# Gate row by column tiles, a new order of the opening, and remainder weight rows in three requests

## The chip, the cores and the metric

The kernel runs on one core of one Trainium2 chip. The metric is the device time of one execution in microseconds (us). TensorE (PE in the profile) multiplies, PEld is its weight load, VectorE is DVE, ScalarE is ACT, GpSimd is POOL, and SyncE (SP) issues most of the transfers (DMAs).

## What is computed

```python
mod = (silu(c) @ w_mod).reshape(1, 6, 1, 576)     # sa, ca, ga, sb, cb, gb
h = layernorm(x) * (1 + ca) + sa
x = x + ga * attention(h)      # 32 heads of 18; 8 keys per position, 2 apart, backwards
h = layernorm(x) * (1 + cb) + sb
x = x + gb * (((h @ w_gate) * (h @ w_up)) @ w_down)   # 576 -> 4608 -> 576
```

x has 2048 rows of 576 columns; everything is bfloat16 with float32 sums.

## The kernel before, in words

The 2048 rows are cut into 8 chunks of 256 rows (two halves j of 128). The attention of a chunk is: layernorm, transpose, q, k and v (`a_q`, `a_v`), products of q with shifted k (`b_p`, in the opening `pj`), their sums by head (`b_l`, `lj`), a softmax over 8 positions, and the weighted sum of shifted v. v goes to DRAM (`vd`) and comes back shifted (`b_ld`). For chunk 0 alone the shift is made on TensorE: `shift_attn` shifts the attention weights, `av_mul` multiplies, `av_sum` shifts back and adds. Half 1 needs 16 rows of half 0 as well: constants `edge` and `edge_t`, the weights `ash_e` and the values `v_e`.

The MLP works on groups of chunks, [[0], [1, 2], [3, 4], [5, 6], [7]]. `gate_up` loops over f, 36 tiles of 128 hidden columns; `down` multiplies by w_down. 576 = 4 x 128 + 64, so the last 64 rows of w_gate and w_up, the remainder rows, are kept apart in `wgr`: gate in partitions 0 to 63, up in 64 to 127, 4608 columns each, loaded by `load_wgr` (L158) in two requests of 64 rows. A `Pair` (L708, its matmuls are issued by L706) runs gate on the lower 64 rows of TensorE and up on the upper 64 at the same time, then swaps. The other 512 rows come in blocks of 4 f (`load_wgu`, L146): blocks 0 to 2 in the opening, block 3, used from f = 12, into the tile hh.

What sets the order: every engine and every DMA queue does its instructions in the order of the code, and they wait for each other by semaphores. The opening (L1020 to L1218) is an order written out by hand. From `gate_up` on, pieces of the next chunks' attention are put between the f tiles by a planner (`timed`), from costs and due times in tuples: (TensorE cost, VectorE cost, needs, mark, wait, call).

The change touches these places. `mod_row` (L349) makes a row ga or gb, copied to all 128 partitions by a 128-column stationary operand: 5 matmuls of 512 columns, 5 of 64, two ScalarE copies to float32 (L358, L359). ga is made in the opening from `wmC`; gb in the first `gate_up`, from `wm5` and `wm5r`. `mod_columns` (L321) makes the other rows by four matmuls at a time, each in 32 columns of the array. `sum_j` (L1090) is softmax's sum, reciprocal and product for a half of chunk 0. `b_wj` (L577) is chunk 0's output projection. `norm_act` (L283) is a layernorm on ScalarE. `pet` (L1143) are seven small matmuls that turn `edge` into `edge_t`.

Of the kernel before, what the change touches and what calls it, by code (L numbers as in the profile page):

```python
# [18 lines left out]
P = 128  # L19
# [9 lines left out]
FT = FF // P  # L29
HALO = 16  # L30
# [8 lines left out]
VR = H - VA  # L39

# [4 lines left out]
def kernel(  # L45
# [31 lines left out]
    vstage = pool("vstage", 2)  # L77
# [25 lines left out]
    ga_bc = consts.tile([P, D], F32, name="ga_bc")  # L103
    gb_bc = consts.tile([P, D], F32, name="gb_bc")
# [4 lines left out]
    wgr = wts.tile([P, FF], BF, name="wgr")  # L109
# [5 lines left out]
    vd = dramp.tile([HALO + S, D], BF, name="vd")  # L115
    prod_t = consts.tile([P, 4 * KT * CH], BF, name="prod_t")
# [41 lines left out]
    def load_wgr():  # L158
        for t, wsrc in enumerate((B_w_gate, B_w_up)):
            r = nc.sync.dma_start(wgr[64 * t:64 * (t + 1), :], wsrc[KF * P:D, :])  # L160
        return r
# [66 lines left out]
    for k in range(2):  # L228
# [11 lines left out]
    edge = sp.tile([HALO, W - 1, P], BF, name="edge")  # L240
# [4 lines left out]
    nc.gpsimd.affine_select(out=edge[:], in_=edge[:], compare_op=ALU.not_equal, fill=1.0, base=-2,  # L245
                            pattern=[[-(HALO + DIL), W - 1], [1, P]], channel_multiplier=-1)
    nc.gpsimd.affine_select(out=edge[:], in_=edge[:], compare_op=ALU.is_ge, fill=0.0, base=SPAN - 1,
                            pattern=[[-DIL, W - 1], [0, P]], channel_multiplier=-1)
    nc.gpsimd.memset(wo[64:, KF, :], 0.0)
# [10 lines left out]
    def ln_parts(src, tag, act=False, both=None):  # L260
        stats = small.tile([P, ST, 2, 6], F32, name="ln_stats" + tag)
        mv = small.tile([P, ST, 2], F32, name="ln_mv" + tag)
        rstd = small.tile([P, ST], F32, name="ln_rstd" + tag)
        xn = xns[turn[0] % 2]
        turn[0] += 1
        both = tag == "b" if both is None else both

        def stat(j, hfs=(0, 1)):
            for hf in hfs:
                nc.vector.bn_stats(stats[:, j, hf, :], src(j)[:, hf * 288:(hf + 1) * 288])  # L270
            if hfs[-1] == 1:
                nc.vector.bn_aggr(mv[:, j, :], stats[:, j, :, :].rearrange("p a b -> p (a b)"))

        def rsq(r):
            nc.scalar.activation(rstd[:, r], mv[:, r, 1], ACTF.Ln, bias=eps[:])
            nc.scalar.activation(rstd[:, r], rstd[:, r], ACTF.Exp, scale=-0.5)

        def norm(j):
            for d0, s0, n in ((0, 0, D), (D, D - 64, 64))[0:2 if both else 1]:
                nc.vector.tensor_scalar(xn[:, j, d0:d0 + n], src(j)[:, s0:s0 + n], mv[:, j, 0:1], rstd[:, j:j + 1],  # L280
                                        ALU.subtract, ALU.mult)

        def norm_act(j):  # L283
            nb = small.tile([P, 1], F32, name="ln_nb")
            nc.vector.scalar_tensor_tensor(nb[:], mv[:, j, 0:1], -1.0, rstd[:, j:j + 1], ALU.mult, ALU.mult)
            for d0, s0, n in ((0, 0, D), (D, D - 64, 64))[0:2 if both else 1]:
                nc.scalar.activation(xn[:, j, d0:d0 + n], src(j)[:, s0:s0 + n], ACTF.Identity, bias=nb[:], scale=rstd[:, j:j + 1])
        return xn, stat, rsq, (norm, norm_act) if act is None else norm if not act else norm_act
# [60 lines left out]
    def mod_row(wm, dst):  # L349
        pa = ps([P, 512], F32, "pa")  # L350
        pb = ps([P, 64], F32, "pb")
        for p_t, c0, c1 in ((pa, 0, 512), (pb, 512, D)):
            for kt in range(KT):
                m = wm(kt)
                rows = slice(0, m.shape[0])
                nc.tensor.matmul(p_t[:], lhsT=sc_bc[rows, kt, :], rhs=m[:, c0:c1],
                                 start=(kt == 0), stop=(kt == KT - 1))
        nc.scalar.copy(dst[:, 0:512], pa[:])  # L358
        nc.scalar.copy(dst[:, 512:D], pb[:])  # L359
# [176 lines left out]
    def shift_attn(j):  # L536
        pz = ps([P, W, H], F32, "pz")
        for w in range(W):
            o = SPAN + DIL * (W - 1 - w)
            nc.tensor.matmul(pz[:, w, :], lhsT=shifts[:, o:o + P], rhs=attn0[:, j, w, :], start=True, stop=True)  # L540
        ashs[j] = sp.tile([P, W, H], BF, name=f"ash{j}")
        nc.scalar.copy(ashs[j][:], pz[:])
        if j > 0:
            pzb = ps([P, H], F32, "pzb")
            for w in range(W - 1):
                nc.tensor.matmul(pzb[:], lhsT=edge[:, w, :], rhs=attn0[0:HALO, j, w, :], start=(w == 0), stop=(w == W - 2))
            nc.scalar.copy(ash_e[:], pzb[:])
        bb[0]["vsh"][j] = vshp.tile([P, W, DH, H], BF, name="vsh")
# [9 lines left out]
    def av_sum(j, hf, acc={}):  # L558
        if hf == 0:
            acc[j] = (ps([P, KF, P], F32, "po"), ps([P, P], F32, "po4"))  # L560
        po, po4 = acc[j]
        v = bb[0]["vsh"][j][:].rearrange("p w d h -> p w (d h)")
        dst = [(po[:, m, :], m * P) for m in range(KF)] + [(po4[:], D - P)]
        for w in range(4 * hf, 4 * hf + 4):
            o = SPAN - DIL * (W - 1 - w)
            for m, (d, c0) in enumerate(dst):
                nc.tensor.matmul(d, lhsT=v[:, w, c0:c0 + P], rhs=shifts[:, o:o + P], start=(w == 0 and m in (0, KF)),  # L567
                                 stop=(w == W - 1), skip_group_check=True)
        if hf == 1:
            if j > 0:  # L570
                for d, c0 in dst:
                    nc.tensor.matmul(d[:, 0:HALO], lhsT=v_e[:].rearrange("p d h -> p (d h)")[:, c0:c0 + P], rhs=edge_t[:],
                                     start=False, stop=True, skip_group_check=True)
            nc.scalar.copy(oT[:, 0:KF, js(j)], po[:])
            nc.scalar.copy(oT[0:64, KF, js(j)], po4[64:P, :])

    def b_wj(j):  # L577
# [10 lines left out]
        def rest(stat):  # L588
            for hf, (cs, pw) in enumerate(pws):
                nc.vector.tensor_tensor(xt[:, cs], pw[:], ga_bc[:, cs], ALU.mult)  # L590
                nc.vector.tensor_tensor(xt[:, cs], xt[:, cs], x_res[0][:, j, cs], ALU.add)
                stat(j, (hf,))
        return rest
# [138 lines left out]
    def wg_pair(gi, hh, f, part):  # L732
# [6 lines left out]
        def side(t):  # L739
            def ops(rows, k):  # L740
                if k == KF:
                    return wgr[rows, js(f)], ht[rows, KF, :]
# [18 lines left out]
        return Pair(("pg", "pu"), N, (side(0), side(1)), finish)  # L761
# [253 lines left out]
    def load_wm5():  # L1015
        nc.gpsimd.dma_start(wm5(), w_mod[0:KF * P, 5 * D:6 * D].rearrange("(k p) n -> p k n", p=P))
        nc.gpsimd.dma_start(wm5r[0:64, :], w_mod[KF * P:D, 5 * D:6 * D])
# [70 lines left out]
    ashs = {}  # L1088

    def sum_j(j):  # L1090
        ss = small.tile([P, H], F32, name="ssj")
        nc.vector.tensor_reduce(ss[:], dd0[:, j].rearrange("p w h -> p h w"), axis=AX.X, op=ALU.add)
        nc.vector.reciprocal(ss[:], ss[:])
        nc.vector.tensor_tensor(attn0[:, j], dd0[:, j], ss[:, None, :].to_broadcast([P, W, H]), ALU.mult)

    load_wm(wmC, 2, 1)
    for dd4 in range(4):
        nk = (DH - dd4 + 3) // 4
        wsrc = bass.AP(A_wo.tensor, A_wo.offset + dd4 * D, [[DH * D, H], [4 * D, nk], [1, D]])
        nc.sync.dma_start(wo[dd4 * H:(dd4 + 1) * H, 0:nk, :], wsrc)  # L1100
    load_res(0)
    load_wm_tail(wmB, 3)
    nc.sync.dma_start(wmB[:, 0:KF, :], w_mod[0:KF * P, 3 * D:5 * D].rearrange("(k p) n -> p k n", p=P))
    load_x(2)
    load_wgr()
    for g in range(3):
        load_wgu(g)
    cp, dv = nc.scalar.copy, nc.vector.tensor_copy
# [32 lines left out]
    pet = ps([P, HALO], F32, "pet")  # L1141
    for w in range(W - 1):
        nc.tensor.matmul(pet[:], lhsT=edge[:, w, :], rhs=ident[0:HALO, 0:HALO], start=(w == 0), stop=(w == W - 2))  # L1143
    nc.scalar.copy(edge_t[:], pet[:])
    mod_row(lambda k: wmC[:, k, :], ga_bc)
    for w in range(4):
        lj(1, w)
    sum_j(0)
    a_q(1, 0)
    shift_attn(0)  # L1150
    for w in range(4, 8):
        pj(1, w)
    a_q(1, 1)
    for w in range(4, 8):
        lj(1, w)
    av_mul(0, 0)
    max_j(1)
    a_q(1, 2)
    av_mul(0, 1)
    sum_j(1)  # L1160
    a_q(1, 3)
    av_sum(0, 0)
    a_q(1, 4)
    av_sum(0, 1)
    shift_attn(1)
# [3 lines left out]
    xn2, stat2, rsq2, norm2 = ln_parts(lambda j: x1[0][j], "b")  # L1169
    stat2c(0)  # L1170
    stat2c(1)
    rsq2c(slice(0, 2))
    av_mul(1, 0)
    x1_halves = []

    def products_1():
        x1_halves.append(b_wj(0))
        norm2c(0)
        norm2c(1)
        a_v(1, 0)  # L1180

    add_modc = mod_columns(wmB, 1, products_1)
    x1_half = x1_halves[0]
    av_mul(1, 1)
    edge_mul()
    add_modc()
    av_sum(1, 0)
    x1_half(stat2)
    a_t(2, False)
    av_sum(1, 1)  # L1190
    b_p(1, 0)
    rsq2(slice(0, 1))
    a_v(1, 1)
# [17 lines left out]
    a_v(2, 0)  # L1211
    b_l(1, 0)
    for w in range(4, 8):
        b_p(1, w)
    a_v(2, 1)
# [41 lines left out]
    def gb_row():  # L1257
        mod_row(lambda k: wm5()[:, k, :] if k < KF else wm5r[0:64, :], gb_bc)
# [3 lines left out]
    first = [(0, 0, "", "p17", 1.4, nop), (0.75, 0, "p17", "l14", 1.0, lambda: b_l(1, 4)), (0.35, 0, "l14", "t14", 0.3, lambda: b_lt(1))] + first  # L1262
# [8 lines left out]
               [[(0, 0, "", "-", 0, lambda: (load_wm5(), load_wd(0))), (0, 0, "", "z3", 8.0, both_halves), (0, 0, "", "w5", 12.0, nop), (1.5, 0, "w5", "-", 0, gb_row), (0, 0, "", "-", 0, lambda: load_res(2))],  # L1271
# [3 lines left out]
                                         (0.6, 0.8, "n4 v3", "x4", 0, lambda: (a_t4(), load_x(6)))]]),  # L1275
# [84 lines left out]
```

## Time and profile before

| | us |
|---|---|
| median of 3 runs | 544.71 |
| lowest and highest | 543.72, 546.1 |
| the profiled execution, by its own time | 544.44 |
| its span (first to last instruction) | 542.7 |
| mean granted TensorE clock | 1.00 of full |
| TensorE busy in the first 130 us | 127.44 |
| DMA rate, 24 to 27, 27 to 36 and 36 to 41 us | 415, 217 and 356 GB/s |

How to read it: an engine's busy time is the sum of its instructions' spans; matmul ends are modelled. The chain is followed back from the last instruction, at each step to what released it; its lines give start, length and what ran. A line of waits says who waited for whom, the total, how often. A line of issues gives the tile, the queue, the size and the median time from issue to landing. A queue's line gives packets, megabytes and the share of 16 DMA engines' time. L numbers are lines of the kernel.

### The profile page before, as it was taken

What the parts mean: (1) busy time and instruction counts of PE and PEld (TensorE: products, weight loads), DVE (VectorE), ACT (ScalarE), POOL (GpSimd) and SP (SyncE); (2) the same over time, 40 slices, a digit from 0 to 9 for tenths busy, and PEclk for the clock granted to TensorE, in tenths of its full rate; (3) what the DMA queues carried; (4) which work ended last, traced back from release to release, by engine and by line L of the source; (5) the groups of instructions that cost most, each with busy time, mean ns of one, the idle gap of its engine ahead of it and who ended that gap; (6) DMA issues with size and microseconds to landing.
All of it is one profiled execution on the core that took longest, in us unless ns stands there. A gap on an engine that the chain in (4) does not pass through costs nothing.

```text
span 542.7 us, 14569 instructions
## 1 busy us (share of the span) xinstructions
PE 535.3 (99%) x6157; PEld 321.9 (59%) x6189; DVE 315.9 (58%) x713; ACT 251.5 (46%) x617; POOL 67.9 (13%) x104
## 2 busy tenths in 40 slices
PE   8999999999999999999999999999999999999997
PEld 4887789756745444555544444555544445558875
DVE  4989586777766777646358896524344924032212
ACT  4776777543566553022645552014555551006630
POOL 7104012122000110111000110110010101010210
PEclk9999999999999999999999999999999999999999
DMA  8999999778872694878435983894296592849821
GB/s 264 299 261 363 336 272 332 258 224 258 267 203 89 211 208 153 227 220 293 135 108 163 232 288 68 162 239 159 89 275 176 156 311 69 255 138 294 271 74 42
DMA packets 94924, 114.52 MB, mean 211 GB/s; under 512 B 27980, under 2 KB 83676, under 8 KB 94732
## 3 DMA queue, kind: packets, MB, share of 16 engines
q1 hardware_dynamic: 83360, 67.29, 44.6%
q0 software_dynamic: 11344, 46.25, 27.8%
q8 instruction: 48, 0.79, 0.6%
q14 instruction: 16, 0.13, 0.1%
q10 hardware_dynamic: 156, 0.07, 0.0%
HBM read 103.15 MB, written 4.74 MB: 199 GB/s over the span
## 4 chain that ended last, share of the span: by engine, by line
PE 94%; DMA 3%; DVE 1%; SPq 1%; ACT 1%; issue 0%
PE pg L706 28%; PE pu L706 23%; PE acc L921 19%; PE pq L706 3%; PE accr L926 3%; PE pw L605 3%; PE pq L416 3%; PE acc L976 3%; PE lgT L470 2%; DMA wmC<-in_w_mod_dram 2%; PE pv L706 2%; PE pv L439 1%; DMA wqk<-in_A_wqkv_dram 1%; PE po L567 1%; PE pwj L584 0%
## 5 line engine op out<-in xcount | busy, mean ns | idle before, releaser
L706 PE MATMUL pg<-h2T,wgu 64*128 64x512 bf16 (+1 forms) x1376 | 265.5, 331 | 0.0
L706 PE MATMUL pu<-h2T,wgu 64*128 64x512 bf16 (+1 forms) x1376 | 264.5, 331 | 0.0
L706 PEld LDWEIGHTS <-wgu 64*128 64x128 bf16 x2752 | 136.5, 94 | 94.8 <-issue 0.5
L757 ACT CAST u_sb<-pu 128x512 bf16<-128x512 f32 (+1 forms) x172 | 85.4, 497 | 135.8 <-PE pg L706 131.2
L760 DVE TENSOR_TENSOR hh<-g_sb,u_sb 128x512 bf16<-128x512 bf16 x136 | 57.4, 423 | 116.2 <-ACT g_sb L758 115.7
L758 ACT CAST g_sb<-pg 128x512 bf16<-128x512 f32 (+1 forms) x172 | 86.7, 504 | 0.0
L921 PEld LDWEIGHTS <-hh 128*128 128x128 bf16 x504 | 49.0, 98 | 59.5 <-issue 1.5
L921 PE MATMUL acc<-wd,hh 128*128 128x512 bf16 x329 | 84.1, 380 | 0.1
L926 PE MATMUL accr<-wd,hh 128*128 128x64 bf16 x344 | 62.4, 193 | 0.7
L706 PE MATMUL pu<-h2T,wgr 64*128 64x512 bf16 (+1 forms) x188 | 61.5, 327 | 0.2 <-ACT u_sb L757 0.2
L706 PE MATMUL pg<-h2T,wgr 64*128 64x512 bf16 (+1 forms) x188 | 61.5, 327 | 0.0
L926 PEld LDWEIGHTS <-hh 128*128 128x128 bf16 x504 | 45.8, 98 | 1.9
L171 POOL DMA_DIRECT2D wd<-in_B_w_down_dram x29 | 21.8, 752 | 190.0 <-PE accr L926 93.4
L461 DVE TENSOR_TENSOR prod_t<-qT,kT 128x1280 bf16<-128x1280 bf16 x56 | 43.7, 818 | 0.7 <-ACT kT L777 0.7
L514 DVE TENSOR_TENSOR vsh<-vsh,attn 128x1152 bf16<-128x1152 bf16 x56 | 39.6, 748 | 1.2 <-DMA vsh<-vd 1.2
L706 PEld LDWEIGHTS <-wgr 64*128 64x128 bf16 x376 | 19.7, 94 | 15.4 <-issue 2.5
L921 PE MATMUL acc<-prod_t,hh 128*128 128x512 bf16 x111 | 28.8, 380 | 0.0
L304 ACT ACTIVATE h2T<-h2T,modc 128x256 bf16<-128x256 bf16 x12 | 6.6, 595 | 45.3 <-DMA h2T<-xn 45.3
L455 POOL DMA_DIRECT2D vsh<-vd x14 | 12.5, 897 | 104.8 <-DVE o_sb L524 89.6
L706 PE MATMUL pq<-hT,wqk 64*128 64x256 bf16 (+1 forms) x360 | 22.2, 259 | 0.1
L416 PE MATMUL pq<-hT,wqk 128*128 128x256 bf16 (+1 forms) x225 | 21.2, 251 | 0.4 <-ACT hT L304 0.4
L926 PE MATMUL accr<-prod_t,hh 128*128 128x64 bf16 x112 | 21.6, 193 | 0.1
(208 smaller groups left out, 605.0 us busy)
## 6 DMA issues: line engine op xcount, KB each, us to landing
wgu<-in_B_w_gate_dram SPq DMA_DIRECT2D x41, 512.0 KB, 4.5
wgu<-in_B_w_up_dram SPq DMA_DIRECT2D x41, 512.0 KB, 6.4
wd<-in_B_w_down_dram POOLq DMA_DIRECT2D x29, 576.0 KB, 5.6
vsh<-vd POOLq DMA_DIRECT2D x14, 1152.0 KB, 9.3
prod_t<-in_B_w_down_dram POOLq DMA_DIRECT2D x8, 576.0 KB, 7.6
hh<-in_B_w_down_dram POOLq DMA_DIRECT2D x6, 576.0 KB, 6.4
x_r<-in_A_x_dram SPq DMA_DIRECT2D x8, 288.0 KB, 8.3
vd<-v_sb POOLq DMA_DIRECT2D x16, 144.0 KB, 5.2
```

What stands on the lines that cost most here:

```text
L171: return nc.gpsimd.dma_start(wb[:], B_w_down[r0:r0 + FB * P, :].rearrange("(k p) n -> p k n", p=P))
L416: nc.tensor.matmul(pq[:, gi, :], lhsT=wqk[:, kt, m * P:(m + 1) * P], rhs=hT[:, kt, cols], start=(kt == order[0] and not (by_k and gi)), st ...
L461: nc.vector.tensor_tensor(prod, aa[i]["qT"][:], aa[i]["kT"][:, :, off:off + CH], ALU.mult)
L514: nc.vector.tensor_tensor(v, v, at, ALU.mult)
L605: nc.tensor.matmul(pw[:], lhsT=oT[:, m, js(j)], rhs=wo[:, m, 0:512], start=(m == 0), stop=(m == KT - 1))
L706: return nc.tensor.matmul(out, lhsT=lhs, rhs=rhs, start=first, stop=last, skip_group_check=True)
L757: nc.scalar.copy(u[:, c, :], pu)
L758: nc.scalar.copy(g[:, c, :], pg)
L760: return lambda: nc.vector.tensor_tensor(hh[:, f - c:f + 1, :], g, u, ALU.mult)
L921: nc.tensor.matmul(acc[j][:], lhsT=hh[:, f, js(j)], rhs=wb[:, f % FB, 0:512], start=(f == 0), stop=(f == FT - 1))
L926: nc.tensor.matmul(accr[:, j, :], lhsT=hh[:, f, js(j)], rhs=wb[:, f % FB, 512:D], start=(f == 0 and j == 0), stop=(f == FT - 1), skip_grou ...
L976: nc.tensor.matmul(acc[i][:], lhsT=hh[:, f, js(j)], rhs=wb(f)[:, c0:c1], start=(f == 0), stop=(f == FT - 1))
```

## The change

- The remainder rows: `wgr` becomes [128, 2, 2304]. The gate rows come in one request to all 128 partitions, its source read as 2 column halves x 64 rows x 2304 columns; the up rows in two requests of 64 partitions, with the halves the other way round. It is issued after weight block 1 in place of before block 0. From f = 18 on, up runs on the lower rows of TensorE and gate on the upper.
- gb is made by `gb_cols`: 20 matmuls of 144 columns, four side by side, one copy to bfloat16, then through DRAM (`gd`) and back to all partitions, on GpSimd's queue. ga keeps its way (`ga_row`). Both rows are bfloat16.
- `edge_t` is built on GpSimd by a memset and seven selects, `edge` has 128 rows in place of 16; the `pet` matmuls go.
- The reciprocal in `sum_j` becomes exp(-ln) on ScalarE, and its product is a step of its own, `share_j`.
- `norm_act`'s extra 64 columns go to VectorE.
- The opening from `pj(1, 3)` to `b_ld(1, 0)` has another order; the end of `av_sum` for half 1 is `av_out`; `load_x(2)` is issued before `load_res(0)`; `a_v(2, 1)` stands before `b_l(1, 0)`.
- `vstage` has 4 buffers in place of 2; three numbers of the planner change.

```diff
     def load_wgr():
-        for t, wsrc in enumerate((B_w_gate, B_w_up)):
-            r = nc.sync.dma_start(wgr[64 * t:64 * (t + 1), :], wsrc[KF * P:D, :])
-        return r
+        rows = slice(KF * P, D)
+        nc.sync.dma_start(wgr[:, 0, :], bass.AP(B_w_gate.tensor, B_w_gate.offset + KF * P * FF, [[FH, 2], [FF, 64], [1, FH]]))
+        nc.sync.dma_start(wgr[64:, 1, :], B_w_up[rows, 0:FH])
+        nc.sync.dma_start(wgr[0:64, 1, :], B_w_up[rows, FH:FF])
...
+    nc.gpsimd.memset(edge_t[:], 0.0)
+    for w in range(W - 1):
+        d = edge_t[:, 0:SPAN - DIL * w]
+        nc.gpsimd.affine_select(out=d, in_=d, compare_op=ALU.not_equal, fill=1.0, base=-DIL - (HALO + DIL) * w,
+                                pattern=[[-1, SPAN - DIL * w]], channel_multiplier=1)
...
-            for d0, s0, n in ((0, 0, D), (D, D - 64, 64))[0:2 if both else 1]:
-                nc.scalar.activation(xn[:, j, d0:d0 + n], src(j)[:, s0:s0 + n], ACTF.Identity, bias=nb[:], scale=rstd[:, j:j + 1])
+            nc.scalar.activation(xn[:, j, 0:D], src(j)[:, 0:D], ACTF.Identity, bias=nb[:], scale=rstd[:, j:j + 1])
+            if both:
+                nc.vector.tensor_scalar(xn[:, j, D:], src(j)[:, D - 64:D], mv[:, j, 0:1], rstd[:, j:j + 1], ALU.subtract, ALU.mult)
...
+    def gb_cols(wm):
+        pa = ps([P, GC], F32, "pa")
+        for kt in range(KT):
+            for q in range(4):
+                nc.tensor.matmul(pa[H * q:H * (q + 1), :], lhsT=sc_bc[:, kt, 0:H], rhs=wm(kt)[:, GC * q:GC * (q + 1)],
+                                 start=(kt == 0), stop=(kt == KT - 1), skip_group_check=True)
+        nc.scalar.copy(grow[:], pa[:])
+        nc.gpsimd.dma_start(gd[:], grow[0:P:H, :])
+        nc.gpsimd.dma_start(gb_bc[:], bass.AP(gd.tensor, gd.offset, [[0, P], [1, D]]))
...
-                    return wgr[rows, js(f)], ht[rows, KF, :]
+                    return wgr[rows, t, js(f % (FT // 2))], ht[rows, KF, :]
...
-        return Pair(("pg", "pu"), N, (side(0), side(1)), finish)
+        if f < FT // 2:
+            return Pair(("pg", "pu"), N, (side(0), side(1)), finish)
+        return Pair(("pu", "pg"), N, (side(1), side(0)), lambda pu, pg: finish(pg, pu))
...
-        nc.vector.reciprocal(ss[:], ss[:])
-        nc.vector.tensor_tensor(attn0[:, j], dd0[:, j], ss[:, None, :].to_broadcast([P, W, H]), ALU.mult)
+        nc.scalar.activation(ss[:], ss[:], ACTF.Ln)
+        nc.scalar.activation(ss[:], ss[:], ACTF.Exp, scale=-1.0)
+        sums[j] = ss
...
+    load_x(2)
     load_res(0)
     load_wm_tail(wmB, 3)
     nc.sync.dma_start(wmB[:, 0:KF, :], w_mod[0:KF * P, 3 * D:5 * D].rearrange("(k p) n -> p k n", p=P))
-    load_x(2)
-    load_wgr()
     for g in range(3):
         load_wgu(g)
+        if g == 1:
+            load_wgr()
...
-    pet = ps([P, HALO], F32, "pet")
-    for w in range(W - 1):
-        nc.tensor.matmul(pet[:], lhsT=edge[:, w, :], rhs=ident[0:HALO, 0:HALO], start=(w == 0), stop=(w == W - 2))
-    nc.scalar.copy(edge_t[:], pet[:])
-    mod_row(lambda k: wmC[:, k, :], ga_bc)
+    a_q(1, 0)
+    ga_row()
+    sum_j(0)
     for w in range(4):
         lj(1, w)
-    sum_j(0)
-    a_q(1, 0)
+    pj(1, 4)
+    pj(1, 5)
+    share_j(0)
+    a_q(1, 1)
     shift_attn(0)
...
+    x1_halves[0](stat2, edge_mul)
+    a_tiles(2)
+    hT2 = aa[2]["hT"]
+    ev2 = transposed(xn2c, lambda m: hT2[:, m, :], (0, 1), 0)
+    av_out(1)
+    ev2(False)
...
-    first = [(0, 0, "", "p17", 1.4, nop), (0.75, 0, "p17", "l14", 1.0, lambda: b_l(1, 4)), (0.35, 0, "l14", "t14", 0.3, lambda: b_lt(1))] + first
+    first = [(0, 0, "", "p17", 2.2, nop), (0.75, 0, "p17", "l14", 1.0, lambda: b_l(1, 4)), (0.35, 0, "l14", "t14", 0.3, lambda: b_lt(1))] + first
```

## The prediction

> **What bounds the kernel now.** I read the page's busy times first, then the chain, then the opening in the timeline and the transfers in the same stretches.
>
> ```profile
> span 542.7 us, 14569 instructions
> PE 535.3 (99%) x6157; PEld 321.9 (59%) x6189; DVE 315.9 (58%) x713; ACT 251.5 (46%) x617; POOL 67.9 (13%) x104
> ...
> PE 94%; DMA 3%; DVE 1%; SPq 1%; ACT 1%; issue 0%
> ```
>
> TensorE is busy for 99% of the span and carries 94% of the chain, at a granted clock of 1.0. So a change gains only what it takes off TensorE's own list or out of its few waits, and loses whatever new wait it gives TensorE. The chain from 20 us on, cut to its places of interest:
>
> ```profile
> 11.76 8.89 DMA wmC<-in_w_mod_dram
> 20.65 0.14 issue
> 20.79 0.38 PE pa L356
> ...
> 57.40 1.20 ACT xn L287 x2
> 58.60 0.26 ACT u_sb L757
> ...
> 62.77 0.32 PE pa L356
> ...
> 64.42 0.09 PE pu L706
> 64.50 0.13 PE pg L706 x2
> 64.64 0.28 PE pu L706
> ```
>
> Three waits stand there: for wmC until 20.79, for ScalarE's norm of chunk 3 (the next matmul starts 0.45 us after the one before it, at 58.90, where 0.11 is usual: 0.34 lost), and at 64.64, where the up half of weight block 3 has just landed. The waits name the last one, and the issues give the age of that load:
>
> ```profile
> PEld L706 <- DMA hh<-in_B_w_up_dram: 0.3, 1, 0.3
> ...
> hh<-in_B_w_up_dram SPq DMA_DIRECT2D x1, 512.0 KB, 22.9
> ```
>
> Issued at 41.67, it lands at 64.6 after 22.9 us: the queue is full. So from about 28 to 65 us the transfers keep step with TensorE with nothing to spare, and their order and speed count. The issue sections and queue lines of the first 60 us show two more things:
>
> ```profile
> q10 hardware_dynamic: 12, 0.00, 0.0%
> ...
> vd<-v_sb POOLq DMA_DIRECT2D x6, 144.0 KB, 6.0
> ...
> v_e<-vd POOLq DMA_DIRECT2D x1, 144.0 KB, 10.8
> ```
>
> q10 has carried only the three c_row requests by then. One has a leading count of 4, two of 1. Twelve packets are 6 of data and 6 of completion, 4+1+1 of each. Over the whole page q10 has 156: the 144 more are the last output request, 128 rows and 16 completions. So a request occupies as many DMA engines as its leading count allows, 16 for 128 rows. v_e is written to 128 partitions, but its source leads with a count of 8: in the packet records never more than 8 of its 32 packets are in flight (13 to 16 for vd's), and it needs 10.8 us where vd's requests of the same size need 6.0. The smaller leading count of the two sides decides.
>
> **The remainder rows.** Before, wgr comes as two requests of 64 rows by 9216 bytes. Their 128 packets mean 655 ns in the records, 5.2 us on each of 16 engines; the first ones, few in flight, take 347 ns. From 27 to 36 us the transfers mean 217 GB/s, from 36 to 41 us 356. Writing half of the partitions is slow, and this the change wants to mend. But the new gate request reads its source as [2][64][2304]: a leading count of 2 against 128 partitions. By the c_row and v_e rows it runs on 2 engines. Each gets 64 packets of 4608 bytes, one at a time. The rows for 4608 bytes are 174 ns (half of 347), 178 (vd) and 208 (weight blocks); I take 178: 64 x 178 = 11.4 us. The two up halves add 8 packets to every engine, 1.4 us at 178, 2.8 if half height doubles them. So two engines carry 12.8 us for wgr where they carried 5.2: **7.6 us later** for all that stands behind on this queue, and each later request is complete only when these two engines are. Ends: 11.4 + 1.4 less 5.2 less 2 us, if the dip to 279 GB/s at 61 us is free time, 5.6; at 208 ns and 2.8, 10.9.
>
> The Trainium skill bears on this twice, and its two rules speak against each other here. "DMA: Bandwidth & Descriptors", section "Rules for kernel authors", advises one 128-partition transfer in place of two halves; the 217 GB/s agree, and by that rule alone the time would be the first rival's below. The same page, section "Why a DMA increments its semaphore by 16 and not by 1", gives the engine count as the largest number up to 16 that divides both sides' slowest dimension above 1; the c_row and v_e counts agree, and by that rule the time is the forecast's.
>
> Who waits: behind wgr on SP's queue stand block 2 (wanted about 57.5), x_t of chunk 3 (VectorE's statistics start on it at 50.55, and all its later products queue behind them) and block 3. Block 3 lands at 64.6 + 7.6 = 72.2 in place of 64.6, and TensorE stands there, or in part earlier at block 2. Since these engines are full from 28 to 65, the sum at f = 12 is the same wherever the first wait falls. What TensorE gains before f = 12 is given back there.
>
> **The opening.** TensorE drops pet (7 matmuls, 20.32 to 20.65). They lay in the wait for wmC, and a_q(1,0), whose input is complete at 20.36, now fills this place: 20.32 to 20.79, 0.47 gained. pzb at full height: 0.27 to 7 x 0.027 = 0.19 in the chain, 0.08. Against it, the two steps 1/sum move from VectorE (0.35 each) to ScalarE (Ln 0.30 + Exp 0.20 with the hand-over), behind the copies of ga_bc, which now end near 23.4. Walking the three queues in order with these rows, share_j(0) ends near 24.5, just when a_q(1,1) does: shift_attn(0) waits 0.1 to 0.35, shift_attn(1) up to 0.1, b_wj(0) up to 0.2 for oT. Net 0.1 gained (bounds 0.35 lost, 0.4 gained). load_x(2) goes ahead of wmB, which then lands near 30 in place of 28.8; its reader comes near 31.5, so nothing, and without that cover about 1 us. VectorE comes out some 0.5 to 1 us later, covered by a_v(2,1) moved ahead of b_l(1,0).
>
> **GpSimd.** edge_t costs one memset and 7 selects: at most 0.35 each by the 128x156 select (0.31), and edge's 0.83 + 0.97 + 0.97 at full height stay near that by the 128x256 memset (0.32). That is 2.6 us on a queue that then sits 6.3 us idle before its first vd store: nothing. The memset before wm5 (0.57) delays gb's weights to 61.5; they are read from 62.7: nothing.
>
> **The gate row gb.** Before, 10 matmuls from 62.77 to 64.42, 1.6 us. After, 20 of 144 columns, four side by side. Nearest rows: 20 of 320 columns in the same arrangement took 0.90 (pm), 20 of 32 columns 0.49 to 0.55 (lgj). I take 0.65: 0.95 gained (0.7 to 1.1). The row's trip through DRAM on GpSimd's queue (two requests, 6 us each by the vd row) is read first at 127.4: nothing; block wd 3, queued behind, is used after 98.
>
> **The rest.** The 64-column norm moves from ScalarE (0.43) to VectorE, twice for chunk 3: the 0.34 at 58.90 goes. bf16 ga_bc and gb_bc: the products read PSUM, and PSUM-fed VectorE work takes 0.69 for 512 columns with one operand (kT) or two (o_t): nothing. From f = 18 on, the sides swap engine rows and copies: same counts, nothing. vstage with 4 buffers only allows a_v(1,0) to go earlier.
>
> **The sum.** Up to f = 12 the gains are 0.1 + 0.34 + 0.95 = 1.4; the wait there takes them and 7.6 more. After f = 12 nothing changes. The profiled execution took 544.44 (span 542.7 and 1.7 around it), 0.3 below the median of 544.71. 544.4 + 7.6 = **552.0**, with 550.0 to 555.3 by the bounds, and 547 to 556 if SP's blocked queue or the late x_t takes more or less.
>
> **Rivals.**
> First, the gate request is spread over 16 engines after all, since the lowering might recut its source. For it: only requests of GpSimd and ScalarE show the rule here, none of SP's. Then wgr costs 64 packets x 2 of 178 ns plus 128 halves of 347 over 16 engines, about 4.2 us, 1.0 less than before; block 3 lands some us earlier since it gets ahead of GpSimd's large loads, its 0.27 wait goes, and all gains stay: 0.1 + 0.34 + 0.95 + 0.27 = 1.6, **542.8** (bounds 540.5 to 544).
> Second, it does run on two engines but block 3 and x_t come in time, because those engines have idle time that the mean over 16 hides. Against it: the means over 5 us stay at 333 to 374 GB/s from 35 to 60 us. Then **544**.
> Third, the opening's new order itself is late: shift_attn(0) behind the ga_bc copies at 0.35, x_t(2) and wmB at 1 us, with no gain at f = 12: **545**, still within what can be told.
>
> **Chances.** 0.5%, 2.7 us, is about what a measurement of this kernel can tell from no change. Two engines and a wait: 0.60, all slower. Sixteen engines: 0.28; a busy TensorE has modelled ends and may hide waits that go too, so 0.12 of it below 541.7 and 0.16 within. Hidden: 0.07, late opening: 0.05, both within. So faster 0.12, same 0.28, slower 0.60. The range takes in both groups, 542.2 to 556: it leaves out the 0.12 below and some 0.08 above. The likeliest case alone has 547 to 556.
>
> **What would show it.** wgr's gate request landing 12 us or more after its engines reach it (11.2 before with full queues), SP's issues of block 2 blocked longer, VectorE idle on x_t near 52 us, a TensorE wait on a wgu or hh load between 48 and 72 us; gb's matmuls in about 0.65 us; no pet; a wait of 0.1 to 0.35 before pz. If the rate stays above 340 GB/s from 34 us on and block 3 lands before 62, the forecast is wrong and the first rival right. If wgr lands late and TensorE doesn't wait, the second.

## The result and the profile after

The changed kernel takes **561.03 us** (median of 6, 559.61 to 562.48) against 544.07 for the kernel before, a ratio of 1.0309, interval [1.0294, 1.0325]. The forecast was 552.0 with a range of 542.2 to 556: slower, as forecast, but by 17 us in place of 7.6. Ratios, here and below, are taken over the executions within 1.5% of each kernel's fastest, medians and ranges over all of them. The page of the profiled execution begins so:

```profile
span 558.0 us, 14552 instructions
...
PE 539.1 (97%) x6192; PEld 321.9 (58%) x6192; DVE 316.4 (57%) x715; ACT 250.2 (45%) x615; POOL 71.1 (13%) x115
...
PE 88%; DMA 6%; DVE 3%; ACT 1%; SPq 1%; issue 0%
```

TensorE now has some 19 us without work, where it had 7, and transfers hold 6% of the chain in place of 3%. Where that is, a table of stretches shows (start:end, length, then busy us of each engine, the granted clock, the mean DMA share and GB/s):

```profile
45.00:50.00 5.00, 3.87 (x50) 2.35 (x47) 4.26 (x9) 4.73 (x14) 1.68 (x3) 1.00 1.01 289
50.00:55.00 5.00, 0.00 (x0) 0.00 (x0) 1.93 (x3) 0.00 (x0) 0.92 (x2) 0.86 1.02 297
55.00:60.00 5.00, 2.63 (x23) 1.69 (x25) 0.00 (x0) 0.00 (x0) 2.10 (x3) 0.50 0.72 206
60.00:65.00 5.00, 5.00 (x93) 3.76 (x91) 0.42 (x1) 2.83 (x9) 0.00 (x0) 0.96 1.03 331
65.00:70.00 5.00, 3.92 (x71) 3.25 (x68) 1.73 (x6) 1.42 (x5) 0.00 (x0) 1.00 0.74 218
70.00:75.00 5.00, 1.86 (x26) 1.56 (x27) 4.48 (x11) 2.91 (x9) 0.00 (x0) 0.91 0.94 278
75.00:80.00 5.00, 5.00 (x91) 3.57 (x89) 2.93 (x6) 3.08 (x9) 0.61 (x1) 0.75 1.37 261
```

TensorE stands twice, near 49 to 57 and near 68 to 74, and after each stand its clock is low (0.50, later 0.75). Idle time in these rows is 12.7 us; the slow clock costs another 2.9 by an estimate, each row's busy time times the part of the clock that is missing (2.63 x 0.50 + 5 x 0.04 + 1.86 x 0.09 + 5 x 0.25). The waits name the two stands, TensorE's and VectorE's:

```profile
PE pg L735 <- DMA wgr<-in_B_w_gate_dram: 7.2, 1, 7.2
PE pu L735 <- ACT u_sb L786: 4.2, 2, 2.1
PE pu L735 <- DMA wgr<-in_B_w_up_dram: 1.3, 1, 1.3
```

```profile
DVE ln_statsa L281 <- DMA x_t<-in_A_x_dram: 5.4, 1, 5.4
```

The first is the new gate request. The second goes over x_t of chunk 3: SP's own timeline (start, length of the issue) shows why it is late, and the chain what hangs on it.

```profile
27.32 0.64 SPq L165 DMA_DIRECT2D wgr<-in_B_w_gate_dram  x1
28.01 2.80 SPq L166 DMA_DIRECT2D wgr<-in_B_w_up_dram  x1
...
33.49 9.54 SPq L158 DMA_DIRECT2D wgu<-in_B_w_up_dram  x1
43.13 12.55 SPq L140 DMA_DIRECT2D x_t<-in_A_x_dram  x1
```

```profile
43.13 25.05 DMA x_t<-in_A_x_dram
68.20 0.83 DVE ln_statsa L281 x2
...
73.12 0.87 ACT xn L297
73.99 0.26 ACT u_sb L786
74.30 0.37 PE pu L735
```

SP needs 9.5 and 12.6 us to issue one request each, and x_t lands at 68.2 where it landed at 46.8 before. By f = 12 the kernel is 14.7 us behind (its first matmul with wgr at 78.94 against 64.22), and at the first w_down matmul 14.6. So all but 0.6 of the 15.3 us by which the spans differ lie ahead of f = 12.

### The profile page after: what moved, and what is told of

Same layout as the page of the kernel before. It is cut to its first block, busy times and chain, and to the rows that moved or that the text cites. A ratio compares the mean times of both kernels' runs of the same rounds, so it can differ in the third digit from the quotient of the medians.

```text
span 558.0 us, 14552 instructions
## 1 busy us (share of the span) xinstructions
PE 539.1 (97%) x6192; PEld 321.9 (58%) x6192; DVE 316.4 (57%) x715; ACT 250.2 (45%) x615; POOL 71.1 (13%) x115
## 4 chain that ended last, share of the span: by engine, by line
PE 88%; DMA 6%; DVE 3%; ACT 1%; SPq 1%; issue 0%
PE pg L735 24%; PE pu L735 24%; PE acc L952 20%; DMA x_t<-in_A_x_dram 4%; PE pw L634 3%; PE accr L957 3%; PE acc L1007 3%; PE pq L735 2%; PE pq L435 2%; PE pv L735 2%; PE lgT L489 1%; DMA wqk<-in_A_wqkv_dram 1%; PE pv L458 1%; PE po L589 1%; DVE ln_statsa L281 0%; DVE vsh L533 0%
## 5 line engine op out<-in xcount | busy, mean ns | idle before, releaser
L735 PE MATMUL pg<-h2T,wgu 64*128 64x512 bf16 (+1 forms) x1376 | 268.4, 334 | 0.0
L952 PE MATMUL acc<-wd,hh 128*128 128x512 bf16 x344 | 86.0, 380 | 0.0
L952 PEld LDWEIGHTS <-hh 128*128 128x128 bf16 x504 | 48.9, 98 | 59.4 <-issue 1.3
L957 PE MATMUL accr<-wd,hh 128*128 128x64 bf16 x344 | 62.4, 193 | 0.0
L177 POOL DMA_DIRECT2D wd<-in_B_w_down_dram x29 | 21.8, 752 | 166.3 <-PE accr L957 93.7
```

What stands on the lines that cost most here:

```text
L177: return nc.gpsimd.dma_start(wb[:], B_w_down[r0:r0 + FB * P, :].rearrange("(k p) n -> p k n", p=P))
L735: return nc.tensor.matmul(out, lhsT=lhs, rhs=rhs, start=first, stop=last, skip_group_check=True)
L952: nc.tensor.matmul(acc[j][:], lhsT=hh[:, f, js(j)], rhs=wb[:, f % FB, 0:512], start=(f == 0), stop=(f == FT - 1))
L957: nc.tensor.matmul(accr[:, j, :], lhsT=hh[:, f, js(j)], rhs=wb[:, f % FB, 512:D], start=(f == 0 and j == 0), stop=(f == FT - 1), skip_grou ...
```

## The experiments

Ratios are to the kernel before on the same chip (543.8 to 544.1 us). Where executions scatter, their range says more than the ratio, and one profiled execution may not stand for the rest.

| kernel | us, median (range) | ratio and interval |
|---|---|---|
| e1 gate in two halves | 550.69 (547.5 to 556.0) | 1.0107 [1.0079, 1.0135] |
| e2 before, with new wgr alone | 562.76 (562.3 to 563.6) | 1.0343 [1.0330, 1.0356] |
| e3 x_t(3) ahead of wgr | 561.96 (558.1 to 562.1) | 1.0305 [1.0276, 1.0334] |
| e4 halves cut into 62 + 2 rows | 561.29 (560.6 to 562.0) | 1.0314 [1.0301, 1.0328] |
| e5 e1 + pad on GpSimd | 553.72 (545.6 to 554.5) | 1.0102 [1.0045, 1.0159] |
| e6 e1 + old gb row | 550.34 (548.3 to 557.6) | 1.0104 [1.0087, 1.0122] |
| e7 e1 + pet matmuls back | 552.38 (546.6 to 555.1) | 1.0118 [1.0078, 1.0159] |
| e8 e5 + planner's old numbers | 546.00 (544.8 to 547.5) | 1.0039 [1.0024, 1.0054] |
| e9 e5 + wd block 3 early | 547.69 (546.9 to 549.8) | 1.0064 [1.0048, 1.0080] |
| e10 e8 and e9 together | 546.91 (545.5 to 549.2) | 1.0050 [1.0032, 1.0068] |
| e11 before, new planner numbers | 546.67 (545.9 to 547.3) | 1.0049 [1.0034, 1.0064] |
| e12 before, new opening | 545.94 (545.2 to 546.7) | 1.0032 [1.0020, 1.0045] |
| e13 e10 + wd behind block 3 | 553.04 (548.1 to 555.9) | 1.0150 [1.0108, 1.0192] |
| e14 before + wd behind block 3 | 549.40 (545.3 to 551.0) | 1.0089 [1.0062, 1.0116] |
| e15 before, new gb row | 545.89 (544.8 to 546.8) | 1.0035 [1.0024, 1.0046] |

### e1 to e4: the gate request

e1, in the changed kernel, cuts the gate request into two of 64 rows:

```diff
-        nc.sync.dma_start(wgr[:, 0, :], bass.AP(B_w_gate.tensor, B_w_gate.offset + KF * P * FF, [[FH, 2], [FF, 64], [1, FH]]))
+        for h in range(2):
+            for r0, r1 in ((0, 64),):
+                nc.sync.dma_start(wgr[64 * h + r0:64 * h + r1, 0, :], B_w_gate[KF * P + r0:KF * P + r1, h * FH:(h + 1) * FH])
```

> The changed kernel with one edit: the gate remainder comes in two requests of 64 rows (left columns to partitions 0 to 63, right columns to 64 to 127) in place of the one whose source leads with a count of 2. Theory A (that request runs on two DMA engines and everything behind it waits): no wait on wgr, x_t of chunk 3 lands before 50 us, 542.8 us, between 540.5 and 544. Theory B (the opening's new order, with VectorE and ScalarE later, is what costs): 553 us or more, the first gate matmul still late by several us.

e2 is the kernel before with the change's `load_wgr`, its place in the queue and the swapped sides, nothing else.

> The kernel before with the remainder rows alone changed (three requests, after weight block 1, sides swapped from f = 18). Theory A: 558 to 563 us, wgr's gate request lands near 56 us, the first gate matmul waits 7 us for it and VectorE 15 us or more for x_t of chunk 3. Theory B: 543 to 546 us.

e3 is the changed kernel with `load_x(3)` issued ahead of `load_wgr()`.

> The changed kernel with x_t of chunk 3 issued ahead of the remainder rows in place of behind weight block 2. If the loss has two parts, TensorE's wait for wgr at f = 0 and VectorE's wait for x_t, then the first stays (7 to 9 us) and the second goes: 551 to 555 us. If the late x_t alone makes the loss: 545 or less. If the first wait alone makes it, or block 2 or 3 takes the place of x_t: 558 to 562.

e4 is e1 with each 64-row half in requests of 62 and 2 rows.

> The gate remainder in requests of 62 and 2 rows for each column half, so no source is recut, but the leading count of both sides is 62, and the largest divisor up to 16 of 62 is 2. Theory A in its strong form (the engine count is the largest number up to 16 that divides the leading counts): the same two engines with 62 packets each, 556 to 563 us, gate landing 50 to 57 us. Rival (a count below 16 is the limit, or the recut source is slow for another reason): 541 to 544 us, as with 64 rows.

e2 has the whole loss by itself: 18.6 us over the kernel before. It shows the same two stands (the list of waits):

```profile
DVE ln_statsa L273 <- DMA x_t<-in_A_x_dram: 19.1, 1, 19.1
...
PE pg L709 <- DMA wgr<-in_B_w_gate_dram: 6.1, 1, 6.1
```

e4 tells why the request is slow. With a leading count of 64 the same bytes cost 550.7, with 62 they cost 561.3, and TensorE stands for 13.0 us at wgr:

```profile
PE pu L737 <- DMA wgr<-in_B_w_up_dram: 13.0, 1, 13.0
```

62 has no divisor up to 16 above 2. The packet records show the same: from 41 us on never more than three of wgr's packets are in flight in the changed kernel and in e4, and the last end at 58.8 and 62.3, where in e1 the last has ended at 41.7. So a request runs on as many engines as the largest number up to 16 that divides its leading counts on both sides. The Trainium skill, "DMA: Bandwidth & Descriptors", section "Why a DMA increments its semaphore by 16 and not by 1", gives this rule, and e1 and e4 agree with it.

e3's time is the one expected if the first wait alone made the loss, but that isn't what its trace shows. VectorE no longer waits for x_t, and the first stand grows from 7.2 to 12.0 us: the gate request's packets start at 35.5 in place of 34.1, and TensorE gets wgr at 61.3 in place of 56.1. Why they also take longer no run shows. The waits don't add up; the order only decides which of them is seen. e1 missed: neither 542.8 nor 553 and up, but 550.7. The 10.3 us are the gate request's, and 6.6 us are left of which TensorE's waits in the changed kernel show nothing: what is found next falls within its first stand, 48.9 to 56.1.

### e5 to e7: where GpSimd's code is fetched

In e1 TensorE has weights and x_t in time, but it waits 1.8 us at gb's row. GpSimd's timeline in e1 (the brackets hold the idle time ahead of an instruction):

```profile
51.15 0.57 POOL L1049 MEMSET o_t<- 64x576 bf16 x1
57.59 0.76 POOL L1050 DMA_DIRECT2D hh<-in_w_mod_dram  x1 [5.87 <-PE pg L737]
```

The kernel before issues this load, gb's weights, at 50.77. In the packet records a packet of 8192 bytes on the instruction queue q14 starts at 55.63, 2.0 us ahead of the load. The releaser in the brackets is the last event ahead of the load and not its cause: the changed kernel's own line for this load has 5.67 us and none, and e5 and e7 below issue it without the wait.

```diff
+    pad = sp.tile([P, 1], BF, name="pad")
+    for _ in range(10):
+        nc.gpsimd.memset(pad[:], 0.0)
```

> Gate request as two 64-row halves, and ten one-element memsets more on GpSimd in its idle time at the start. Theory A: GpSimd's instructions are fetched in blocks of 128 (8 KB packets of queue q14), and the change has pushed a block's end to the place between the memset of wm5r and the load of wm5, where the fetch takes 5.9 us because all DMA engines are full (packet at 55.54, load at 57.59). Ten instructions more push the block's end back into GpSimd's wait of 12.5 us from 29.8 to 42.3, so the load of wm5 is issued within 0.5 us of its memset, near 51.7; the wait of TensorE at gb's row goes; 542.5 to 545.5. Theory B: the memset or the new gb row itself delays the load: it stays near 57.6, time 550 to 551.5.

e6 has, in e1, the ten matmuls, the two copies and the 64-row load of the kernel before for gb, with its old cost in the planner:

> Gate request as two 64-row halves, and gb's row made as in the kernel before: no memset of wm5r, no trip through DRAM. Theory A: in GpSimd's list the load of wm5 stands at place 68 in place of 69, the block's end at 64 stays ahead of it, so it is still issued 5 to 6 us after the vd store ahead of it, near 57, and the time stays at 549 to 553 (gb's 20 short matmuls, some 1 us, are lost as well). Theory B: the load is issued at 51 to 52 and the time comes to 543 to 545.

e7 has, in e1, no memset and selects for edge_t on GpSimd, but the seven `pet` matmuls.

> Gate request as two 64-row halves, and edge_t made by seven small matmuls as in the kernel before, so that GpSimd's list is 15 instructions shorter; memset, load and gb row as in the changed kernel. Theory A: the load of wm5 stands at place 54, ahead of the block's end at 64, and is issued near 51.7; the fetch then falls among the loads of wd at about 75 to 85 us, whose data is used after 98; 543 to 546. Theory B: load near 57.6, 550.5 to 552.

The load goes where theory A has it in all three. First e5, then e6, which has no memset at all and still stands:

```profile
51.61 0.57 POOL L1052 MEMSET o_t<- 64x576 bf16 x1
52.13 0.76 POOL L1053 DMA_DIRECT2D hh<-in_w_mod_dram  x1
```

```profile
49.70 1.16 POOL L467 DMA_DIRECT2D vd<-v_sb  x2
56.84 0.76 POOL L1049 DMA_DIRECT2D hh<-in_w_mod_dram  x1 [5.99 <-PE pu L737]
```

e7 issues it at 50.97. So the 5.9 us belong to a place in GpSimd's list of instructions, not to an operation: the load stands as number 68 (e6) and 69 (e1, the changed kernel), waits included and counted from 0, and does not as number 54 (e7, the kernel before) and 79 (e5). The 15 instructions that edge_t adds moved it there. That the stand is the fetch of the next block of instructions is inferred from the q14 packet, which starts 1.8 to 2.0 us ahead of the load in the changed kernel, e1 and e6 (54.78, 55.63, 54.92). In e5 it starts at 47.45, not in the earlier wait that I expected, and 2.1 us behind it comes a vsh load, 0.7 us later than in e1. The Trainium skill, "Runtime: NRT & Kernel Launch", section "Instruction fetch mechanics", has such a fetch in 16 KiB blocks and mostly hidden. Here the packets have 8 KB and, with the DMA engines full (a share of 1.08 from 50 to 55 us in e1), 5.9 us were not hidden.

The times of e5 and e7 missed: they should have come to 542.5 to 546 and scatter from 545.6 to 555.1. In the profiled executions the wait for gb's weights falls from 1.8 us to 0.4 in e5 and to nothing in e7, and most of what is left comes later. At f = 12 (the first up matmul on block 3) e1 is 2.9 us behind the kernel before, e5 1.7 and e7 not at all; at the first w_down matmul 5.7, 3.9 and 10.4. So a third thing was under the second.

### e8 to e11: two transposes beside GpSimd's loads

e7's profiled execution (555.06, its longest) loses its time at 80 to 105 us (same columns as above):

```profile
90.00:95.00 5.00, 4.26 (x75) 3.38 (x70) 3.01 (x6) 2.67 (x8) 0.00 (x0) 1.00 0.96 290
95.00:100.00 5.00, 1.19 (x16) 0.75 (x13) 2.19 (x5) 2.02 (x5) 0.00 (x0) 0.95 1.03 341
```

In the packet records 4608-byte packets of GpSimd's queue (0.2 us each as a rule) take 3.3 to 6 us at 76 and 85, at the time of SP's transposes lg_t; in e1 (550.72) they take 3.1 to 4.0 us at 84 to 85. The transposes land late (median from issue to landing): the kernel before, then e1, then e7:

```profile
lg_t<-lgs SPq DMA_TRANSPOSE x2, 5.2
```

```profile
lg_t<-lgs SPq DMA_TRANSPOSE x2, 13.6
```

```profile
lg_t<-lgs SPq DMA_TRANSPOSE x2, 17.1
```

In e6 it is 15.3, in e5 9.7. The instruction lists suggest the reason: in the kernel before SP's transposes stand ahead of weight blocks 6 and 7, in e1, e5, e6 and e7 behind them. Two of the planner's numbers (p17's wait 2.2, gb's cost 0.85) differ; e6, which has gb's old cost 1.5, has the new order too, so there it is p17's wait.

```diff
-    first = [(0, 0, "", "p17", 2.2, nop), ...
+    first = [(0, 0, "", "p17", 1.4, nop), ...
...
-               (0.85, 0, "w5", "-", 0, gb_row)
+               (1.5, 0, "w5", "-", 0, gb_row)
```

> The padded kernel with two gate halves (545.6 to 554.5 from run to run), and two of the planner's three numbers as in the kernel before (p17's wait 1.4, gb's cost 1.5). Theory C: the new numbers put SP's two transposes lg_t behind weight blocks 6 and 7 in place of ahead of them, so that they run at the same time as GpSimd's loads of wd, and then packets of both hang for 1.5 to 8 us and TensorE waits for weights at 80 to 100 us. With the old numbers the transposes go ahead again: no packet over 1.5 us at 80 to 100, TensorE busy over 4.8 of 5 us in every stretch from 75 on, 542.5 to 545, and a spread of under 1.5 us between runs. Theory D: the load of wd block 3, which the trip of gb's row holds back from 53 to 72 us, is what collides with the transposes: still 545 to 554.

```diff
     def gb_row():
+        ld_d1(3)
         gb_cols(lambda k: wm5()[:, k, :] if k < KF else wm5r[:])
-        ld_d1(3)
```

> The padded kernel with two gate halves, and only the load of wd block 3 issued ahead of gb's row in place of behind its trip through DRAM; the planner's new numbers stay. Theory C: the transposes still run beside the wd loads issued near 80, 546 to 554 with a wide spread. Theory D: no collision near 76 or 84, 542.5 to 545.

> Both edits together (planner's two numbers as before, wd block 3 ahead of gb's row), with the pad and the two gate halves. By either theory nothing is left to wait for: what remains of the change is its gain on TensorE, 0.47 for a_q in place of pet, 0.34 for the norm and 1.0 for gb's row less what the last waits keep: 542 to 543.5.

> The kernel before, with only the planner's three numbers of the change (2.2, 0.85, 0). Theory C: the transposes move behind weight blocks 6 and 7 as in the changed kernel and hang beside the wd loads: 547 to 553, with a spread of some us. Theory D: wd block 3 is still loaded at 53 us, so nothing collides: 543.5 to 545.

With the old numbers e8 takes 546.0 and scatters by 2.7 us in place of 8.9. That is 7.7 us below e5's median and 3.4 by the ratios; between the two profiled executions it is 2.8. So the new numbers cost time, as theory C has it, but late transposes with stuck packets are seen in the traces of e1, e6 and e7 alone. In e8 lg_t still lands after 8.7 us, and no trace was kept of e5's four executions of 553 to 554.5. With the three new numbers alone the kernel before takes 2.8 us more (e11, 0.3 under what I expected), and there late transposes are not the cause: lg_t lands after 6.3 us, and 2.3 us are lost by f = 12, when no transpose lg_t has been issued yet. Of these, 1.2 are there at f = 0 already, ahead of anything that the planner orders, and 0.9 are a wait of TensorE at 63.4 that is put down to VectorE:

```profile
PE pu L706 <- DVE ln_nb L285: 0.9, 1, 0.9
```

A wait of 0.9 put down to VectorE ahead of f = 12 stands in e1, e5, e7 and e9 as well, which have the new numbers, and not in e8, e10 and the kernel before. In e9 and e11 the second lg_t runs beside GpSimd's loads of wd, as in e1, and lands after 6.9 and 6.3 us: such a pair doesn't hang each time, and what decides it is not shown. e9's ratio lies between e5's and e8's, so the load of wd block 3 may have a part as well; with the old numbers it has none (e10 is no better than e8). e8 and e10 missed too, by 1 and 3.4 us: 2 to 3 us over the kernel before are still there.

### e12 to e15: why nothing is gained

> The kernel before with the change's opening only (order, edge_t on GpSimd, Ln and Exp, the norm's 64 columns on VectorE, load_x(2) first), with the pad on GpSimd; remainder rows, gb's row and the planner's numbers as before. Theory E: all DMA engines are full until weight block 3 lands at about 64.6, so what TensorE gains before f = 12 (0.1 to 0.8) is waited off there: 543.2 to 544.3. Theory F: the opening itself is late and is what keeps the repaired kernels 2 us above the kernel before: 545 to 546.5.

e13 (in e10) and e14 (in the kernel before) hold two loads of w_down back until weight block 3 has landed:

```diff
-               lambda: (load_wm5(), load_wd(0))
+               lambda: (load_wm5(), behind(load_wd(0), wgu_in[3]))
```

> The kernel of the last batch with both edits (545.5 to 549), and the loads of wd blocks 0 and 3 (1152 KB, issued near 53 us, used after 98) held back until weight block 3 has landed. Theory E: 1152 KB at 350 GB/s are 3.3 us, so block 3 lands near 61.5 in place of 64.5, TensorE no longer waits at f = 12 and keeps what it gained before: 541.8 to 543.2, if the two loads, which then run at 62 to 69 us, don't hang beside the transposes hT at 66 to 70; if they do, packets over 1.5 us show there and the time is 545 to 549. Theory F: no earlier end, 545 to 547.

> The kernel before with the same hold of wd blocks 0 and 3. Theory E: block 3 lands near 61.5, but only 0.3 us of waiting is there to win: 543.3 to 544.0; if the held loads hang beside the transposes, 545 to 548.

e15 is the kernel before with `gb_cols`, its memset and its trip, wd block 3 ahead of it:

> The kernel before with the change's gb row only (20 short matmuls, memset, the trip through DRAM on GpSimd's queue), wd block 3 ahead of it and the planner's numbers as before; the load of wm5 stands at place 54 of GpSimd's list, ahead of the block's end at 64. Theory E: 1.0 us less of TensorE work ahead of f = 12 is waited off at f = 12 where block 3 lands: 543.4 to 544.3. If the trip itself (gb_bc from gd, 147 KB, read row by row by 128 partitions) delays the transposes or the weights beside it at 70 to 80: 545 to 546.5, with TensorE waits on wgu after 65. If the gain isn't waited off: 542.7 to 543.2.

e15 shows where 1 us of saved TensorE work goes. It stands as a new wait at f = 12, and block 3 lands 0.8 us later than before (TensorE goes on at 65.4 against 64.6):

```profile
PE pu L719 <- DMA hh<-in_B_w_up_dram: 1.4, 1, 1.4
```

In e12 it is another matter. Block 3 is there by 62.4, and f = 12 still begins at 64.7, as before: no gain is waited off there. The first matmul with wgr starts at 48.97 against 48.83, and two things lie under that. From the first matmul for v to this one e12 takes 32.13 us where the kernel before takes 32.72 and e14 and e15, with the old opening too, 32.53: the new order gains 0.4 to 0.6, and eight more runs with it have the same 32.1. But e12's first matmul for v starts at 16.84 against 16.11, behind waits for the first weights (wmA, wqk). With the old opening it starts between 16.11 and 16.71, with the new one between 16.43 and 17.72; whether the new opening causes that is not shown. e14 turns it round. Without the two loads in its way, block 3 has landed at 60.4 in place of 64.6 (GpSimd's timeline, the held load starts when it has landed):

```profile
60.38 0.80 POOL L171 DMA_DIRECT2D wd<-in_B_w_down_dram  x1 [8.22 <-DMA hh<-in_B_w_up_dram]
```

and TensorE goes through f = 12 without a wait. So in the kernel before the transfers up to block 3 set that point as much as TensorE does. The held loads then run beside the transposes hT, which land late, first the kernel before, then e14 (e13 has 14.8):

```profile
hT<-xn SPq DMA_TRANSPOSE x2, 5.2
```

```profile
hT<-xn SPq DMA_TRANSPOSE x2, 13.5
```

e14 is 5.5 us above the kernel before, e13 9.1 (6.1 above e10): the other branch of what I expected, and 1.4 and 4 us beyond its ranges. In e14's profile the loss comes between f = 12 and the first w_down matmul (5.3 us behind there), where TensorE waits for hT and then runs at half clock from 78.1 to 81.5. This is the cleanest measure here of what a transpose beside GpSimd's loads can cost.

e12 and e15 are 2.0 us slower, which theory E did not give; the times are those of the other branches, but the waits on wgu that e15's branch named do not show. Their profiled executions are 1.0 and 0.8 above the kernel before's, and all of it is there at the first w_down matmul (99.1 and 98.9 against 98.1). In e15 it is block 3, 0.8 us late. In e12 TensorE's weight loads wait 0.4 us for a weight block and 0.4 for hT between 65 and 99. The rest, about 1 us in the medians, stays open, and so does what is left in e8 and e10. No version here beats the kernel before.

## Why the prediction was wrong

The sign and the place were right: the leading count of 2, the two DMA engines, block 2 blocked on SP's queue, the late x_t, TensorE's wait. The step that failed is "**7.6 us later** for all that stands behind on this queue": the gate request took 21.8 us where 11.4 were put, x_t behind it came 21.4 late, and at f = 12 14.7 us were lost.

- **"64 x 178 = 11.4 us"** for the gate request. In the packet records its packets run from 34.1 to 55.9, 21.8 us, and 178 ns holds for only part of them. Up to 40.7 some 37 of the 128 get through, with wgr's packets at 342 ns in the mean; GpSimd's queue has almost none then, and the half-height up rows run on the other engines with packets as long. From 41 to 47 it is 181 ns, as forecast. From 47 to 56 it is 250 ns with GpSimd's vsh packets in between, and as a rule the next one on an engine starts only 420 later. What makes the first part slow is not shown. The bound of 208 ns was no bound, since every row that I took it from was of a request on 16 engines.
- **"The sum at f = 12 is the same wherever the first wait falls."** e3 confirms the fold (a wait moved, no time gained), but the sum is not 7.6. x_t came 21.4 us late, and after TensorE's first stand VectorE and ScalarE still had the whole norm of chunk 3 ahead of them. Block 3 was not the last to come.
- **The clock** was not in the sum. Of the 15.6 us in the table of stretches (12.7 idle and 2.9), 2.9 are the granted clock of 0.5 to 0.75 after the two stands.
- **The gains given back at f = 12**: right for gb's row, as e15 shows (1.4 us of new waiting). The opening's "net 0.1 gained" is 0.1 lost at f = 0 in e12's profile: 0.6 gained behind the first matmul for v and 0.7 lost ahead of it, the latter perhaps by chance. gb's 20 matmuls take less than the 0.65 that I put (the chain in the changed kernel), and it doesn't matter:

```profile
78.04 0.43 PE pa L374 x20
```

- **"GpSimd: nothing."** Wrong, though unseen in the changed kernel, where the gate request covers it. I counted 2.6 us of work in idle time, but not that 15 more instructions move gb's load to a place in the list where GpSimd stands for 5.9 us.
- **"Three numbers of the planner change"** I did not cost at all. With them the kernel before takes 2.8 us more (e11), 0.9 of that in a wait that e1, e5, e7 and e9 show as well; in e5 two of them cost 3.4 by the ratios, 7.7 between the medians.
- **The rivals.** The first, 16 engines, gave 542.8. e1 is that kernel: 550.7. The second (hidden) falls with e2. The third, an opening that is late by itself, 545, is what e12 measures: 545.9. The wait ahead of pz that I gave for it doesn't show; in its profile 1.0 us is lost behind f = 12 and nothing by then.

A range to 556 held neither the longer packets nor a second stand behind the first.

## What to carry to other kernels

Before a request's shape is changed, read its leading count on both sides: here it set the number of engines, and those few were shared with other queues' packets, so that the request took 21.8 us and not the 11.4 of a free engine. Where a wait is taken away and the time doesn't follow, look for the next one under it; here three lay one below the other. Where the transfers set a point that all work must pass, work saved ahead of it is worth nothing (e15), and a changed cost in a planner is a changed order of the queues.

## What the runs showed of the hardware

- SP stands at a request while those ahead of it are stuck on two engines: 9.54 and 12.55 us for one issue each, where 1.9 and 1.3 were needed before.
- TensorE stands from 48.9 to 56.1 in the changed kernel, and the granted clock is 0.50 from 53.6 to 60.4: it falls while TensorE still stands and stays low for 4.3 us after work starts again. After the two waits of 2.1 us near 70 and 73 it is 0.50 again from 74.1 to 77.5.
- Transposes issued by SP at the same time as GpSimd's 576 KB loads land after 13.5 to 17.1 us in place of 5.2 in e1, e6, e7, e13 and e14, with packets of both that take 3 to 8.5 us; in e9 and e11 they land after 6.9 and 6.3. The Trainium skill, "DMA: Bandwidth & Descriptors", section "Rules for kernel authors", says that a transpose next to ordinary DMAs needs nothing. That is a rule for its data; in time it cost 5.5 us in e14, where only the start of two loads was changed.
- GpSimd stands for 5.7 to 6.0 us at number 68 or 69 of its list of instructions, with the DMA engines full. That it waits there for its next block of code is inferred from an 8192-byte packet on q14 about 2 us ahead of its next instruction.
